# Four one-bank PSUM tiles, in a pool opened after the attention, in place of two two-bank tiles for the first product of an MLP

## The chip, the core and the metric

The kernel runs on one core of a Trainium2 chip. TensorE (PE) multiplies, VectorE (DVE) and ScalarE (ACT) do the elementwise work, GpSimd (POOL) and SyncE (SP) issue transfers. The metric is device time in microseconds, as the median of several runs; a profile is one execution of the same program, read instruction by instruction.

## The reference, cut to what matters

```python
def _attn_ref(u, v, z):                       # u, v: (4, 3008, 256), z: (4, 3008, 64)
    scores = (1.0 / S) * np.matmul(z, z.transpose(0, 2, 1))
    attn = np.maximum(scores, 0.0) ** 2
    return u * np.matmul(attn, v)

def _moe_ref(x, w_in, w_out):                 # x: (12032, 256), w_in: (256, 2048), w_out: (2048, 256)
    h = x @ w_in
    g = np.where(h > 0.0, h, np.exp(np.minimum(h, 0.0)) - 1.0)
    return g @ w_out
```

The result of the attention is the input of the MLP.

## The kernel before

Every matrix product is done in three fp32r products of high and low parts (high by high, high by low, low by high). The kernel has two stages on the same engines.

The **attention** takes 288 steps. It writes its scores alternately into two PSUM tiles, `banks[0]` and `banks[1]` (f0 and f1 in the trace, L120); each is 128 x 2 x 512 numbers of 4 bytes, which is two PSUM banks. Four more tiles of one bank each, `accs` (acc), hold the sums over the steps (L121). That makes eight banks, all there are.

The **MLP** takes 96 steps, in 12 groups of 8. A group has the tokens of two blocks side by side: groups 0, 3, 6 and 9 work on 512 columns, the other eight on 496. A step makes two 128-row slices of the hidden layer for both blocks at once by a scheme with seven products in place of eight (`PARTS`), so it has seven first products M1 to M7 of three matmuls each (L508), and eight second products y0 to y7 of three matmuls each (L525 to L527): 45 matmuls.

The MLP takes over the four banks of f0 and f1. `chain` (L495) says which: p is one half of f0, the other half in the next step; q is the first half of f1 and r the second. In one step:

- p takes M1, then M6, M7 and M4 are added to it. ACT copies p out after each of the four: `s1`, `d`, `u3`, `C21` (all L133).
- q takes M2. DVE adds it in `C11` (L583).
- r takes M5; DVE reads that in `C22` (L585). Then M3 is added to r, and DVE reads the sum in `C12` (L587).

From the four results h, of 4 x 496 columns, ACT makes `m` (L589), `T` (L591) and `E` (L593), DVE makes `tt` (L595) and `max` (L597) and splits the hidden layer into parts with `hi` (L602) and `lo` (L130); the y products read those.

The order on each engine is written out by hand, in `PERIOD` with a lag in steps for each entry, and kept as written (`manual_schedule`). It gives, with t the step of the loop:

- PE: M1(t), y4, y0, M2(t), y1, M6(t), M5(t), y2, y6, M7(t), y7, y5, M4(t), y3, M3(t), the y being those of step t-3.
- DVE: C12(t-1), max(t-2), hi(t-2), lo(t-2), C22(t), C11(t), tt(t-1).
- ACT: s1(t), m(t-1), d(t), T(t-1), u3(t), E(t-1), C21(t).

So C12 of the last step stands behind M2 of this one in the program. Waits between engines are made by the framework, tile by tile: an instruction that reads or writes a tile waits for the earlier ones that wrote or read that tile.

The inputs of the MLP come back from DRAM through POOL's queue (L471), three of the seven tiles of a group in the last step of the group before. Step 1 of the MLP also holds the last work of the attention: DVE finishes the last block and splits seven tiles (L449, L450) between max and C11.

Of the kernel before, what the change touches and what calls it, by code (L numbers as in the profile page):

```python
# [7 lines left out]
F32 = mybir.dt.float32  # L8
# [26 lines left out]
def relu2_attention_elu_mlp(  # L35
# [13 lines left out]
    P = 128  # L49
# [18 lines left out]
    ps = ctx.enter_context(tc.tile_pool(name="ps", bufs=1, space=bass.MemoryType.PSUM))  # L68
# [48 lines left out]
    }  # L117
    H_ROW, M_ROW, T_ROW, G_ROW, L_ROW = ("row3", "row1", "row2"), ("row5",), ("row6",), ("row0", "row8"), ("row7", "row4")

    banks = [ps.tile([P, 2, 512], F32, name=f"f{i}") for i in range(2)]  # L120
    accs = [[ps.tile([P, 512], F32, name=f"acc{i}{h}") for h in range(2)] for i in range(2)]  # L121

    def cols(k):
        return starts[k % NI], BLOCKS[k % NI], k // NI
# [17 lines left out]
    def v_load(b, p):  # L142
        t = st_ring.next().rearrange("p (c d) -> p c d", c=2)
        r0 = 2 * p * P
        if p < NP - 1:
            nc.sync.dma_start(out=t, in_=v[b, r0:r0 + 2 * P, :].rearrange("(c p) d -> p c d", p=P))
        else:
            nc.sync.dma_start(out=t[:, 0, :], in_=v[b, r0:r0 + P, :])
            for h in range(2):
                nc.sync.dma_start(out=t[h * TAIL:(h + 1) * TAIL, 1, :], in_=v[b, r0 + P:S, :])  # L150
        v_raw[b, p] = t

    def v_split(b, p):
        t = v_raw.pop((b, p))
        o = v_ring.next().rearrange("p (q c d) -> p q c d", q=2, c=2)
        if (b, p) == (0, 1):
            nc.vector.tensor_copy(out=o[:, 0], in_=t)
            sub(o[:, 1], t, o[:, 0])
        else:
            split(o[:, 0], o[:, 1], t)  # L160
        v_t[b, p] = o
# [5 lines left out]
    def l_load(b, g):  # L167
        t = l_raw[b, g] = lr_ring.next()
        i0, n = g * GP * 2 * P, GP
        if g == NG - 1:  # L170
            n -= 1
            e = (NP - 1) * 2 * P
            nc.sync.dma_start(out=t[TOP, n * P:], in_=zz[b, TOP, e:e + P])
            for h in range(2):
                o = n * P + h * TAIL
                nc.sync.dma_start(out=t[BOT, o:o + TAIL], in_=zz[b, BOT, e + P:S])
        src = zz[b, :, i0:i0 + n * 2 * P].rearrange("p (n two w) -> p n two w", two=2, w=P)
        for c, rows in enumerate((TOP, BOT)):
            nc.sync.dma_start(out=t[rows, :n * P].rearrange("p (n w) -> p n w", w=P), in_=src[rows, :, c])
# [12 lines left out]
    def r_load(k):  # L192
        i0, n, b = cols(k)
        t = rraw_ring.next()
        nc.sync.dma_start(out=t[:, :n], in_=zz[b, :, i0:i0 + n])
        r_raw[k] = t
# [138 lines left out]
    def a_front(s):  # L335
        k, p = divmod(s, NP)
        n, b = cols(k)[1:]
        hh, ll = (t[:, :n] for t in r_t[k])
        if s < 2:

            w = [[t[:, (2 * p + c) * P:][:, :P] for c in range(2)] for t in (hh, ll)]
        else:
            o = (p % GP) * P
            w = [[t[:, o:o + P]] * 2 for t in l_t[b, p // GP]]
        f_t[s] = banks[s % 2]
        outs = [f_t[s][:, c, :n] for c in range(2)]
        for i in range(3):
            both(outs, w[i % 2], [ll if i == 2 else hh] * 2, i == 0, YES if i == 2 else NO)
# [32 lines left out]
    def a_back(s, part=slice(None)):  # L381
        k, p = divmod(s, NP)
        n, b = cols(k)[1:]
        hi, lo = (t[:, :, :n] for t in e_t[s])
        vt = v_t[b, p]
        last = p == NP - 1
        if p == 0:
            acc_t[k] = accs
        acc = [[h[:, :n] for h in t] for t in acc_t[k]]

        def w(q, c, d):
            return vt[:, q // 2, c, d * P:(d + 1) * P]

        for c, d, q in products(s < 4, p in (0, NP - 1))[part]:
            if not (last and c == 1):
                x = (lo if q == 1 else hi)[:, c]
                both(acc[d], [w(q, c, d)] * 2, (x, x), p == 0 and c == 0 and q == 0, NO)
            elif q == 0:

                both(acc[d], [w(0, 1, d)] * 2, (hi[:, 1], lo[:, 1]), False, (d == 1, True))  # L400
                if d == 0:
                    both((acc[0][0], acc[1][1]), (w(2, 1, 0), w(2, 1, 1)), [hi[:, 1]] * 2, False, (True, False))
# [55 lines left out]
    def x_slots(j):  # L458
        if j == 0:
            x_t[0], spare[0] = list(range(7)), list(range(7, NX))  # L460
        else:
            x_t[j] = spare[j - 1] + x_t[j - 1][:7 - EARLY]
            spare[j] = x_t[j - 1][7 - EARLY:]
# [30 lines left out]

    def chain(s):  # L495
        n = cols(2 * (s // MS))[1]
        return banks[0][:, s % 2, :n], banks[1][:, 0, :n], banks[1][:, 1, :n]

    def m_part(s, name):
        j, m = divmod(s, MS)  # L500
# [168 lines left out]
    def start_up():  # L669
        warm = hi_ring.next()[:, :512]  # L670
        nc.vector.memset(warm.bitcast(F32), 0.0)
        copy(lo_ring.next()[:, :1], warm[:, :1].bitcast(F32))
        f = banks[0]
        for i in range(WARM):
            both([f[:, c] for c in range(2)], [warm[:, :P]] * 2, [warm] * 2, True, YES)
        hh, ll = r_t[0] = r_tiles(0)
        z0 = r_raw.pop(0)
        nc.vector.tensor_copy(out=hh, in_=z0)
        sub(ll, z0, hh)

    with tc.manual_schedule():
        for j in range(NSUP):
            x_slots(j)
        r_load(0)
        v_load(0, 0)
        l_load(0, 0)
        v_load(0, 1)
        l_load(0, 1)
        v_load(0, 2)
        start_up()  # L690
        v_split(0, 0)
        for t in range(NSTEP):

            k, p = divmod(t, NP)
            if not (k and p == 3) and t != 2:
                a_front(t)
            if k and p == 2:
                a_front(t + 1)
            if t >= 2:
                a_back(t - 2)  # L700
            if t == 2:

                a_front(t)
            a_mid(t)
            if t == 0:
                l_hi(0, 0)
                l_lo(0, 0)
            background(t)
        assert not jobs, sorted(jobs)
        for t in range(MSTEP):  # L710
            for name, lag in PERIOD:
                s = t - lag
                if t == 0:
                    if name == "M6":
                        a_back(NSTEP - 2, slice(6, 12))
                    elif name == "M2":
                        a_back(NSTEP - 2, slice(0, 6))
                    elif name == "M7":
                        a_back(NSTEP - 1, slice(0, 6))
                    elif name == "M4":  # L720
                        a_back(NSTEP - 1, slice(6, 12))
                if s < 0:
                    continue
                m_op(s, name)
                if t == 1 and name == "s1":
                    a_sums(NBLK - 1)
                if t == 1 and name == "C12":
                    a_out(NBLK - 1)
                    j = NSUP - 1
                    for _ in x_parts(j):  # L730
                        pass
                    next(late[1], None)
                    for i in range(7):
                        x_split(j, i, scalar=False)
                j = t // MS + 1
                if t % MS == MS - 1 and name == "M2" and j < NSUP:
                    for i in range(EARLY, EARLY + 2):
                        x_load(j, i)
                if t % MS == MS - 1 and name == "M6" and j < NSUP:
                    for i in range(EARLY + 2, 7):  # L740
                        x_load(j, i)
            if t % MS == 4 and t // MS + 1 < NSUP:
                for i in range(EARLY):
                    x_load(t // MS + 1, i)
        s = MSTEP - 1
        m_op(s, "C12")
        m_op(s - 1, "max")
        for half in (1, 0):
            for name in ("m", "T", "E"):
                m_op(s, name, half)  # L750
        for i in Y_ORDER:
            y_part(s - 2, i)
        m_op(s - 1, "hi")
        m_op(s - 1, "lo")
        for i in Y_ORDER:
            y_part(s - 1, i)
        m_op(s, "tt", 1)
        m_op(s, "max", 1)
        m_op(s, "hi", 1, scalar=True)
        m_op(s, "tt", 0)  # L760
        m_op(s, "lo", 1)
        m_op(s, "max", 0)
        m_op(s, "hi", 0, scalar=True)
        m_op(s, "lo", 0)
        for i in Y_LAST:
            y_part(s, i)
            if i < 4:
                y_out(s, i)
# [32 lines left out]
```

## Time and profile before

| | us |
|---|---|
| median of 3 runs (2079.28 to 2081.58) | 2079.36 |
| the profiled execution, its own time | 2082.21 |
| its span, first to last instruction | 2080.4 |
| PE busy over the span | 2004.1 (96%) |
| DVE busy | 1727.8 (83%) |
| ACT busy | 1439.3 (69%) |
| POOL busy | 51.1 (2%) |

The attention fills about the first 965 us, the MLP the rest. The chain of work that ended last lies for 60% of the span on PE and for 37% on DVE. In the rows below, a matmul's record starts when it starts; its end is modelled, so that records of neighbours overlap, and the distance of two starts tells how fast matmuls follow each other. A bracket at the end of a row is the time for which the engine sat idle just before, and what ended that.

### The profile page before, as it was taken

Reading aid. Unit: us, or ns where it says so; the run is one execution under the profiler, and the core shown is the slowest. Engines: PE = TensorE matmul, PEld = TensorE weight load, DVE = VectorE, ACT = ScalarE, POOL = GpSimd, SP = SyncE. Lnnn points to the kernel's source line nnn. Section 1 sums busy time; section 2 is a strip of 40 time slices with the busy share of each in tenths; the row PEclk is TensorE's granted clock in tenths of the full one; section 3 lists DMA queues with packets and bytes.
Section 4 is the critical chain, followed back from the end, with each engine's and each line's share of the span. In section 5 each row is a group of like instructions: output and inputs, shape, how many; then the busy total and the mean of one; then the engine's idle time right before and its main releaser. Section 6 shows DMA issues by size and latency. Waiting matters only on the chain.

```text
span 2080.4 us, 30855 instructions
## 1 busy us (share of the span) xinstructions
PE 2004.1 (96%) x12828; PEld 1592.4 (77%) x12828; DVE 1727.8 (83%) x1726; ACT 1439.3 (69%) x1520; POOL 51.1 (2%) x88
## 2 busy tenths in 40 slices
PE   9999999999999999998899999999999999999998
PEld 7888888888888888886677777777777777777776
DVE  7888888888788888676788888888888888888887
ACT  7666876677676777675567667676676766766665
POOL 0000000000000000001000000000000000000000
PEclk9999999999999999999899999999999999999999
DMA  3132332143131421225011121111221111122100
GB/s 117 44 104 95 96 115 81 56 135 110 56 121 45 131 84 46 71 75 165 33 30 60 50 71 59 30 60 30 71 73 36 60 30 61 31 80 69 30 20 20
DMA packets 76460, 143.16 MB, mean 69 GB/s; under 512 B 7456, under 2 KB 50208, under 8 KB 76320
## 3 DMA queue, kind: packets, MB, share of 16 engines
q1 hardware_dynamic: 63936, 97.56, 14.2%
q0 software_dynamic: 12096, 43.13, 7.0%
q8 instruction: 100, 1.64, 0.3%
q10 hardware_dynamic: 288, 0.51, 0.1%
q14 instruction: 40, 0.33, 0.0%
HBM read 85.72 MB, written 55.44 MB: 68 GB/s over the span
## 4 chain that ended last, share of the span: by engine, by line
PE 60%; DVE 37%; issue 2%; ACT 1%; DMA 0%; ACTq 0%; DVEq 0%
PE acc L333 34%; DVE row L130 12%; PE f L508 11%; DVE row L597 10%; PE f L333 8%; DVE row L602 6%; DVE row L587 3%; DVE row L583 3%; DVE row L585 3%; PE acc L525 2%; PE acc L526 2%; PE acc L527 2%; DVE row L375 1%; ACT row L374 1%; DVE row L420 1%
## 5 line engine op out<-in xcount | busy, mean ns | idle before, releaser
L333 PE MATMUL acc<-row,x 64*128 64x496 f32 (+1 forms) x6768 | 806.3, 384 | 4.6 <-DVE row L130 4.4
L333 PEld LDWEIGHTS acc<-row,x 64*128 64x128 f32 x6768 | 633.5, 184 | 135.1 <-DVE row L130 9.2
L130 DVE TENSOR_TENSOR row<-row,row 128x992 fp32r<-128x992 f32 (+7 forms) x464 | 613.6, 1326 | 17.2 <-ACT row L133 1.2
L371 ACT ACTIVATE row<-f 128x992 f32<-128x992 f32 (+1 forms) x287 | 289.5, 1009 | 240.9 <-PE f L333 219.0
L133 ACT ACTIVATE row<-f 128x496 f32<-128x496 f32 (+1 forms) x384 | 222.8, 580 | 157.9 <-PE f L508 155.8
L589 ACT ACTIVATE row<-row 128x1984 f32<-128x1984 f32 (+2 forms) x97 | 181.1, 1867 | 197.1 <-DVE row L587 194.9
L375 DVE CAST row<-row 128x992 fp32r<-128x992 f32 (+1 forms) x287 | 195.3, 681 | 135.4 <-ACT row L374 135.3
L374 ACT ACTIVATE row<-row 128x992 f32<-128x992 f32 (+1 forms) x287 | 299.3, 1043 | 8.4
L526 PE MATMUL acc<-row,wo_hi 128*128 128x496 f32 (+1 forms) x768 | 298.8, 389 | 1.8 <-DVE row L130 1.8
L525 PE MATMUL acc<-row,wo_hi 128*128 128x496 f32 (+1 forms) x768 | 299.0, 389 | 0.0
L527 PE MATMUL acc<-row,wo_lo 128*128 128x496 f32 (+1 forms) x768 | 298.6, 389 | 0.0
L508 PE MATMUL f<-x,wi_hi 128*128 128x496 f32 (+1 forms) x768 | 259.1, 419 | 4.9 <-ACT row L133 4.6
L597 DVE SCALAR_TENSOR_TENSOR row<-row,row 128x1984 f32<-128x1984 f32 (+2 forms) x97 | 215.0, 2216 | 0.0
L595 DVE SCALAR_TENSOR_TENSOR row<-row,row 128x1984 f32<-128x1984 f32 (+2 forms) x97 | 214.8, 2214 | 0.0
L508 PEld LDWEIGHTS f<-x,wi_hi 128*128 128x128 f32 x768 | 130.8, 190 | 81.4 <-ACT row L133 66.2
L587 DVE TENSOR_TENSOR row<-f,row 128x496 f32<-128x496 f32 (+1 forms) x96 | 65.3, 680 | 152.4 <-PE f L508 152.4
L591 ACT ACTIVATE row<-row 128x1984 f32<-128x1984 f32 (+2 forms) x97 | 180.0, 1856 | 1.8 <-DVE row L597 1.7
L593 ACT ACTIVATE row<-row 128x1984 f32<-128x1984 f32 (+2 forms) x97 | 180.7, 1863 | 0.1
L526 PEld LDWEIGHTS acc<-row,wo_hi 128*128 128x128 f32 x768 | 145.1, 189 | 31.2 <-DVE row L130 2.1
L525 PEld LDWEIGHTS acc<-row,wo_hi 128*128 128x128 f32 x768 | 144.8, 188 | 30.2 <-DVE row L602 0.2
L527 PEld LDWEIGHTS acc<-row,wo_lo 128*128 128x128 f32 x768 | 145.0, 189 | 29.0
L508 PE MATMUL f<-x,wi_lo 128*128 128x496 f32 (+1 forms) x384 | 150.4, 392 | 0.0
(71 smaller groups left out, 1587.1 us busy)
## 6 DMA issues: line engine op xcount, KB each, us to landing
x<-x POOLq DMA_DIRECT2D x56, 496.0 KB, 4.6
x<-row SPq DMA_DIRECT2D x84, 248.0 KB, 2.0
x<-x POOLq DMA_DIRECT2D x28, 512.0 KB, 4.7
row<-in_v SPq DMA_DIRECT2D x44, 256.0 KB, 2.8
x<-row SPq DMA_DIRECT2D x42, 256.0 KB, 2.1
row<-in_uT SPq DMA_DIRECT2D x16, 496.0 KB, 4.0
x<-high SPq DMA_DIRECT2D x28, 248.0 KB, 2.0
outT<-x SPq DMA_DIRECT2D x14, 496.0 KB, 3.7
```

The source lines that it names most:

```text
L130: nc.vector.tensor_tensor(out=lo, in0=src, in1=hi.bitcast(F32), op=ALU.subtract)
L133: nc.scalar.activation(out=out, in_=in_, func=AF.Copy)
L333: nc.tensor.matmul(out, w[rows], x[rows], start=start, stop=end)
L371: nc.scalar.activation(out=x, in_=f[:, c, :n], func=AF.Relu, scale=1.0 / S)
L374: nc.scalar.activation(out=x, in_=x, func=AF.Square)
L375: nc.vector.tensor_copy(out=hi[:, c, :n], in_=x)
L508: nc.tensor.matmul(o, w, x, start=first and i == 0, stop=i == 2, skip_group_check=not first)
L525: nc.tensor.matmul(o, wh, hi, start=first, stop=False)
L526: nc.tensor.matmul(o, wh, lo, start=False, stop=False)
L527: nc.tensor.matmul(o, wl, hi, start=False, stop=last)
L595: stt(out=t, in0=m, scalar=1.0, in1=t, op0=ALU.add, op1=ALU.mult)
L597: stt(out=h, in0=h, scalar=0.0, in1=t, op0=ALU.max, op1=ALU.add)
```

## The change

The two-bank tiles of the scores come from a pool of their own, which is closed when the attention's loop is done. A new pool is opened there with four tiles of one bank: p0 and p1 (p of even and of odd steps), q and r. They lie on the same four banks and are used in the same way. No instruction is added or removed on an engine, and none changes its place; lines behind L120 move down by two or three.

```diff
-    banks = [ps.tile([P, 2, 512], F32, name=f"f{i}") for i in range(2)]
+    scores = ExitStack()
+    fs = scores.enter_context(tc.tile_pool(name="fs", bufs=1, space=bass.MemoryType.PSUM))
+    banks = [fs.tile([P, 2, 512], F32, name=f"f{i}") for i in range(2)]
...
     def chain(s):
         n = cols(2 * (s // MS))[1]
-        return banks[0][:, s % 2, :n], banks[1][:, 0, :n], banks[1][:, 1, :n]
+        p0, p1, q, r = singles
+        return (p1 if s % 2 else p0)[:, :n], q[:, :n], r[:, :n]
...
         assert not jobs, sorted(jobs)
+        scores.close()
+        fm = ctx.enter_context(tc.tile_pool(name="fm", bufs=1, space=bass.MemoryType.PSUM))
+        singles = [fm.tile([P, 512], F32, name=name) for name in ("p0", "p1", "q", "r")]
         for t in range(MSTEP):
```

What differs is who waits for whom. These are PE's rows from M3 of one step to M2 of the next, in the MLP with 496 columns; a name in brackets is the semaphore of the engine that is waited for (DVE_49 is DVE's, Activation_49 ACT's). Before:

```order
L508 MATMUL f1_98<-x2_11188,x11_10821 128x496 [waits DVE_49]
L508 MATMUL f1_98<-x2_11188,x11_10821 128x496 x2
L508 MATMUL f0_97<-x7_11036,wi_hi_63 128x496 [waits Activation_49]
L508 MATMUL f0_97<-x7_11036,wi_hi_63 128x496
L508 MATMUL f0_97<-x7_11036,wi_lo_64 128x496
L525 MATMUL acc00_99<-row0_10896,wo_hi_65 128x496
L526 MATMUL acc00_99<-row7_10902,wo_hi_65 128x496
L527 MATMUL acc00_99<-row0_10896,wo_lo_66 128x496
L525 MATMUL acc00_99<-row0_10896,wo_hi_65 128x496
L526 MATMUL acc00_99<-row7_10902,wo_hi_65 128x496
L527 MATMUL acc00_99<-row0_10896,wo_lo_66 128x496
L508 MATMUL f1_98<-x8_11038,wi_hi_63 128x496 x2
```

And in the changed kernel:

```order
L511 MATMUL r_10741<-x2_11199,x11_10832 128x496 [waits DVE_49]
L511 MATMUL r_10741<-x2_11199,x11_10832 128x496 x2
L511 MATMUL p1_10739<-x7_11047,wi_hi_63 128x496 x2
L511 MATMUL p1_10739<-x7_11047,wi_lo_64 128x496
L528 MATMUL acc00_102<-row0_10907,wo_hi_65 128x496
L529 MATMUL acc00_102<-row7_10913,wo_hi_65 128x496
L530 MATMUL acc00_102<-row0_10907,wo_lo_66 128x496
L528 MATMUL acc00_102<-row0_10907,wo_hi_65 128x496
L529 MATMUL acc00_102<-row7_10913,wo_hi_65 128x496
L530 MATMUL acc00_102<-row0_10907,wo_lo_66 128x496
L511 MATMUL q_10740<-x8_11049,wi_hi_63 128x496 [waits DVE_49]
L511 MATMUL q_10740<-x8_11049,wi_hi_63 128x496
```

M1 has lost a wait on ACT and M2 has gained one on DVE. Two waits keep their semaphore and change the count that they ask for, in all 96 steps of the built program: M3 asks for the count of C22 of its step, where it asked for that of C11, one instruction later on DVE. C12 of step t-1 asks PE for the third matmul of M3(t-1), where it asked for the third of M2(t), which stands twelve matmuls further on.

## Rows read from the trace of the kernel before

**Rows 1.** Busy time by stretch: attention, the MLP's first steps (two), the steady MLP.

```profile
core 0: us, PE busy (x) PEld busy (x) DVE busy (x) ACT busy (x) POOL busy (x), PEclk, DMA share, GB/s
500.00:960.00 460.00, 457.79 (x4074) 381.27 (x4072) 372.60 (x476) 330.45 (x375) 5.15 (x9) 1.00 0.28 89
975.00:980.00 5.00, 2.27 (x8) 0.97 (x6) 4.17 (x7) 4.01 (x6) 0.00 (x0) 0.96 0.01 2
980.00:985.00 5.00, 3.30 (x6) 1.66 (x6) 4.52 (x10) 4.81 (x5) 0.00 (x0) 0.50 0.35 131
1100.00:1400.00 300.00, 286.19 (x1202) 219.38 (x1202) 255.28 (x187) 203.95 (x199) 15.88 (x25) 1.00 0.18 57
```

**Rows 2.** Waits, 1400 to 1700 us: who for whom; us in total, times, longest.

```profile
DVE row L587 <- PE f L508: 42.8, 27, 1.6
```

**Rows 3.** Timeline, one 496-column step: start, us, engine, line, operation, count, idle before.

```profile
1402.57 0.95 PE L508 MATMUL f<-x,x 128*128 128x496 f32 x3 [0.52 <-DVE row L583]
...
1404.04 0.39 PE L525 MATMUL acc<-row,wo_hi 128*128 128x496 f32 x1
...
1405.83 0.39 PE L508 MATMUL f<-x,wi_lo 128*128 128x496 f32 x1
...
1406.26 0.68 DVE L587 TENSOR_TENSOR row<-f,row 128x496 f32<-128x496 f32 x1 [1.61 <-PE f L508]
...
1408.80 0.56 ACT L133 ACTIVATE row<-f 128x496 f32<-128x496 f32 x1
...
1409.21 0.38 PE L527 MATMUL acc<-row,wo_lo 128*128 128x496 f32 x1
...
1411.01 0.57 ACT L133 ACTIVATE row<-f 128x496 f32<-128x496 f32 x1
...
1411.47 1.86 ACT L593 ACTIVATE row<-row 128x1984 f32<-128x1984 f32 x1
1411.64 0.72 PE L508 MATMUL f<-x,wi_hi 128*128 128x496 f32 x2
...
1412.47 0.67 DVE L585 TENSOR_TENSOR row<-f,row 128x496 f32<-128x496 f32 x1
...
1413.06 0.66 DVE L583 TENSOR_TENSOR row<-f,row 128x496 f32<-128x496 f32 x1
...
1413.64 2.21 DVE L595 SCALAR_TENSOR_TENSOR row<-row,row 128x1984 f32<-128x1984 f32 x1
...
1413.78 0.94 PE L508 MATMUL f<-x,x 128*128 128x496 f32 x3 [0.52 <-DVE row L583]
...
1417.43 0.68 DVE L587 TENSOR_TENSOR row<-f,row 128x496 f32<-128x496 f32 x1 [1.58 <-PE f L508]
```

**Rows 4.** Timeline, one step with 512 columns.

```profile
1289.07 0.96 PE L508 MATMUL f<-x,wt 128*128 128x512 f32 x3 [0.55 <-DVE row L583]
...
1290.56 0.39 PE L525 MATMUL acc<-row,wo_hi 128*128 128x512 f32 x1
...
1292.80 0.69 DVE L587 TENSOR_TENSOR row<-f,row 128x512 f32<-128x512 f32 x1 [1.59 <-PE f L508]
...
1295.78 0.39 PE L527 MATMUL acc<-row,wo_lo 128*128 128x512 f32 x1
...
1300.53 0.74 PE L508 MATMUL f<-x,x 128*128 128x512 f32 x2 [0.55 <-DVE row L583]
```

**Rows 5.** Timeline of PE: M3 of step 3 and M3 of the last step, 95.

```profile
1018.55 0.96 PE L508 MATMUL f<-x,wt 128*128 128x512 f32 x3 [0.54 <-DVE row L583]
...
2055.55 0.94 PE L508 MATMUL f<-x,x 128*128 128x496 f32 x3 [0.55 <-DVE row L583]
```

**Rows 6.** Waits, 960 to 1022 us (the MLP's steps 0 to 3).

```profile
DVE row L587 <- PE f L508: 6.5, 2, 4.4
```

**Rows 7.** Last load of a group on POOL's queue; median time to landing of such loads.

```profile
1419.03 0.53 POOL L471 DMA_DIRECT2D x<-x  x1 [0.82 <-PE f L508]
...
x<-x POOLq DMA_DIRECT2D x28, 512.0 KB, 4.7
```

## The prediction, written before the changed kernel ran

> **What bounds the kernel now.** I began with the busy times by stretch [rows 1]. In the attention PE is busy for 457.79 of 460 us, so nothing there depends on a wait, and the change leaves it alone but for its end. In the steady MLP PE is busy for 286.19 of 300 us, DVE for 255.28 and ACT for 203.95: no engine is full, so a chain through several of them must set the pace. The waits name it: DVE's C12 (L587) waits for a first product of PE (L508) in each of the 27 steps between 1400 and 1700 us, 42.8 us in all or 1.6 us a time [rows 2].
>
> One step of the timeline closes the loop [rows 3]. C12 starts at 1406.26, C11 (L583) ends at 1413.06 + 0.66 = 1413.72, 7.46 us later, and DVE pauses nowhere between. M3 starts at 1413.78; its bracket says that it waited for C11. Then PE does M3, M1, y4, y0 and M2, fifteen matmuls, and the next C12 starts at 1417.43, 3.65 us after M3. Together 7.46 + 0.06 + 3.65 = 11.17 us, which is the length of a step. C12 to C11 on DVE, M3 to M2 on PE, and round again.
>
> Both links are false. M3 writes r, and C11 reads q; C12 reads r, whose last product M3 ended at 1402.57 + 0.95 = 1403.52, yet it starts only at 1406.26, just behind the end of M2's last matmul (1405.83 + 0.39 = 1406.22) [rows 3]. M2 writes q. Since q and r are halves of one tile, each is waited for on account of the other. Step by step, PE waits until DVE is done with q, and DVE waits until PE has rewritten q.
>
> **What the change removes.** With q and r in tiles of their own, the built program has M3 ask for C22 and C12 ask for M3. The loop above is cut at both places. What is next, and how long is a step then?
>
> PE by itself: matmuls follow each other undisturbed from y4's first at 1404.04 to y6's last at 1409.21, which is 23 distances in 5.17 us, 0.2248 us each [rows 3]. 45 of them are 10.12 us. With 512 columns the same stretch runs from 1290.56 to 1295.78, 0.2270 us each, 10.21 us a step, against 1300.53 - 1289.07 = 11.46 now [rows 4].
>
> DVE by itself: a step less its only wait, 11.17 - 1.58 = 9.59 us [rows 3], with 512 columns 11.46 - 1.59 = 9.87 us [rows 4].
>
> ACT and DVE in a ring: C12 is followed on ACT by m, d, T, u3, E, and E by tt on DVE, which stands ahead of the next C12. From C12 at 1406.26 to E's end at 1411.47 + 1.86 = 1413.33, then 0.06 to be seen and 2.21 for tt [rows 3]: 9.34 us.
>
> So PE would be the slowest, if it waits for nothing. I check its waits with M3 at 0 and matmul number i at 0.2248 i, all distances from [rows 3]. M7 (number 30) starts at 6.74, its third ends at 7.58, u3 ends 0.04 + 0.57 later at 8.19. M4 (number 39, at 8.77) needs u3: 0.5 us to spare. C22 needs u3 too: 8.25 to 8.92; the next M3 at 10.12 needs C22: 1.1 to spare. C11 ends at 9.50; M2 (at 10.12 + 12 x 0.2248 - 0.67 = 12.1) carries the wait that is new, on C11: 2.6 to spare, and what is queued behind it on PE is not held up. E starts 0.46 after u3 (1411.47 against 1411.01), at 8.08, and ends at 9.94; tt, which could start at 9.5, waits half a microsecond for it, 10.0 to 12.2. C12 then comes 2.1 us after the next M3. M5 (at 4.72 after its M3) rewrites r and needs C12, done at 2.8: 1.9 to spare. d comes 1408.80 - 1406.26 = 2.54 behind C12 and takes 0.56: done at 5.2, M7 wants it at 6.74. All hold. DVE and ACT have moved back by some 1.6 us against PE, and PE no longer stops.
>
> The other waits: M1 loses a wait on ACT that was long over when M1 followed M3. The pool's closing and opening fall in one place, where PE has attention matmuls between the first products of step 0; I count nothing. Group ends have four more copies on ACT, but its 203.95 of 300 us [rows 1], 7.7 us a step with these copies in, stay below 10.1: nothing. The loads: the last of a group is issued at 1419.03 and lands some 4.7 us later [rows 7]; M3 of the next step, which reads it, starts at about 1424.95 + 11.2 = 1436.1. Of 12 us to spare a faster step takes about two.
>
> **The sum.** From M3 of step 3 at 1018.55 to M3 of step 95 at 2055.55 are 92 steps in 1037.0 us [rows 5], 28 with 512 columns and 64 with 496. After: 28 x 10.21 + 64 x 10.12 = 285.9 + 647.7 = 933.6. Gain 103.4 us.
>
> The first steps are another matter. There DVE also splits the last tiles, PE is busy for 2.27 of 5 us, and its granted clock falls from full (2.4 GHz) to 0.50 (1.2 GHz) [rows 1]. The same false wait costs 6.5 us there in two steps [rows 6]; but at the half clock PE itself may be what bounds them. Between 0 and 6.5 I take 3, the middle, since nothing is nearer to one end. The tail behind the last M3 has no M2 to wait for: nothing. 103.4 + 3 = 106 us. The profiled execution took 2082.21 with a span of 2080.4; that is 1974 for the span, and set against the median of the runs, 2079.36 - 106 = **1973**. I round to 1974, with a trifle for the 11 group ends.
>
> On the profile's face the gain looks smaller. PE's idle time is 13.81 of 300 us [rows 1], which over 1037 us is 48. The brackets say the same: 0.52 before M3 [rows 3]. But a record covers 0.39 us where the next matmul could have started 0.2248 after, so a stall shows 0.17 too short, and the first matmul after it is itself slower. The distances of starts hold nothing of this, and I go by them.
> The Trainium skill, page "Trainium Kernel Development and Optimization", section "Performance Expectations", has a rule for that: matmul busy time is a bad metric, because matmuls are pipelined, and the share of weight loading is a better one. By it the 48 us are no ceiling; by the busy row they are. Here the starts agree with the rule: 11.17 a step against 45 x 0.2248.
>
> **The rivals.**
>
> *Only the idle time shown comes back.* If something that I don't see holds matmuls apart once they are dense, the gain is the 48 us of idle records: 2031. Against it, the 23 undisturbed distances already are dense. 4%.
>
> *DVE or ACT becomes the bound.* With 512 columns DVE's 9.87 is within 4% of PE's 10.21, and M4 has only 0.5 us to spare behind u3. If ACT or DVE runs a few per cent slower beside an unbroken PE, or their order meshes less well than my frame, 0.3 us a step comes back, 28 us in 92 steps: 2002. For it: the tight places. Against it: DVE and ACT do the same instructions on the same banks. 11%.
>
> *The clock.* PE without a pause could be granted less. At the half clock a step is 20.2 us; each microsecond in it loses half a one, and 212 us of it, a fifth of the MLP, eat the gain. With a quarter of the MLP's 960 us at the half clock the time is 1974 + 120 = 2094, slower than before. Against it: in the attention PE is busier than it would be here, 457.79 of 460, at a clock of 1.00, and the clock fell where PE was busy for 2.27 of 5 us [rows 1]. 3%.
>
> *The change doesn't do what it says.* If the waits had been by bank all along, nothing changes: 2079. The row of C12 behind M2 [rows 3] speaks against that plainly. 2%.
>
> **How the numbers follow.** The forecast, 1974, has 80%; its own range is 1964 to 1990: 3.5 us less if the first steps give all of the 6.5, and some more if the half clock there is not granted at all; 16 us more for residues of 0.1 to 0.2 us a step. To leave out no more than 2 in 10 the range reaches over the second rival: 1964 to 2008. A measurement of this kernel can tell about 0.2%, 4 us, from no change. Faster: forecast, shown idle time and second rival, 95%; the same: 2%; slower: 3%.
>
> **What would show it.** Right: C12's wait for PE is gone and tt waits for E (ACT) about half a microsecond; PE has no bracket before M3; M3 follows M3 after 10.1 us with 496 columns and 10.2 with 512; the steady MLP has DVE near 95% busy; the clock there stays at 1.00. Wrong: steps of 10.3 or more with a bracket before M4 or M7 (ACT), or before M3 or M5 (DVE); a clock under 1.00 behind 1021 us; M2 waiting for C11; PE waiting for a load at a group's first steps.

## The result, and the profile after

| us | before | after |
|---|---|---|
| median | 2079.35 | 1968.92 |
| ratio after to before, 95% interval | | 0.946 [0.9442, 0.9479] |
| profiled execution, its own time | 2082.21 | 1969.42 |
| its span | 2080.4 | 1967.6 |
| forecast, with its range | | 1974 (1964 to 2008) |

One of the four executions of the changed kernel took 3952.84 us, for a reason that no trace here shows; the median has it in, the ratio leaves it out.

The changed kernel is 110 us faster, 5.4%. The page of its profile, engines' busy time first (PEld is PE's weight load), then the chain of work that ended last:

```profile
PE 1941.4 (99%) x12828; PEld 1611.5 (82%) x12828; DVE 1728.5 (88%) x1726; ACT 1456.7 (74%) x1520; POOL 50.9 (3%) x88
...
PE 94%; DVE 4%; issue 1%; ACT 1%; DMA 0%; ACTq 0%; DVEq 0%
```

DVE has done the same work (1728.5 us against 1727.8) in a shorter time, and the chain has become PE almost alone: 94% where it was PE 60% and DVE 37%. The steady MLP, in the same columns as [rows 1]:

```profile
1100.00:1400.00 300.00, 300.00 (x1337) 250.76 (x1336) 285.20 (x209) 231.51 (x221) 14.79 (x24) 1.00 0.17 52
```

1337 matmuls in 300 us where there were 1202, without an idle record, at the full clock. What waits there are, from 1100 to 1900 us (who for whom; us in total, times, longest; POOL left out):

```profile
ACT row L135 <- PE p L511: 120.3, 192, 1.3
ACT row L592 <- DVE row L590: 46.2, 69, 1.0
DVE row L598 <- ACT row L596: 33.2, 79, 0.5
ACT x L135 <- PE acc L530: 7.6, 10, 0.8
```

C12 (now L590) waits for nobody, where [rows 2] had 1.6 us a step. DVE's only wait left is tt (L598) for E (L596), and PE has none at all. One step with 496 columns:

```profile
1356.40 2.23 DVE L598 SCALAR_TENSOR_TENSOR row<-row,row 128x1984 f32<-128x1984 f32 x1 [0.45 <-ACT row L596]
1356.53 0.83 PE L511 MATMUL r<-x,x 128*128 128x496 f32 x3
1357.20 0.61 PE L511 MATMUL p<-x,wi_hi 128*128 128x496 f32 x2
...
1357.87 0.38 PE L528 MATMUL acc<-row,wo_hi 128*128 128x496 f32 x1
...
1358.54 0.67 DVE L590 TENSOR_TENSOR row<-r,row 128x496 f32<-128x496 f32 x1
...
1359.20 0.61 PE L511 MATMUL q<-x,wi_hi 128*128 128x496 f32 x2
...
1362.98 0.39 PE L530 MATMUL acc<-row,wo_lo 128*128 128x496 f32 x1
...
1364.56 1.85 ACT L596 ACTIVATE row<-row 128x1984 f32<-128x1984 f32 x1
1364.75 0.67 DVE L588 TENSOR_TENSOR row<-r,row 128x496 f32<-128x496 f32 x1
...
1365.33 0.66 DVE L586 TENSOR_TENSOR row<-q,row 128x496 f32<-128x496 f32 x1
...
1366.31 0.57 ACT L135 ACTIVATE row<-p 128x496 f32<-128x496 f32 x1
...
1366.44 2.23 DVE L598 SCALAR_TENSOR_TENSOR row<-row,row 128x1984 f32<-128x1984 f32 x1 [0.45 <-ACT row L596]
1366.58 0.83 PE L511 MATMUL r<-x,x 128*128 128x496 f32 x3
```

M3 follows M3 after 10.05 us, without a bracket, where [rows 3] had 11.2 and one of 0.52. C12 starts 2.01 us behind M3 (forecast: 2.1) and now ahead of the next M2, which it used to wait for. C22 is over 1.16 us before M3 needs it (forecast: 1.1).

### The profile page after: what moved, and what is told of

Same layout as the page of the kernel before. It is cut to its first block, busy times and chain, and to the rows that moved or that the text cites. A ratio compares the mean times of both kernels' runs of the same rounds, so it can differ in the third digit from the quotient of the medians.

```text
span 1967.6 us, 30854 instructions
## 1 busy us (share of the span) xinstructions
PE 1941.4 (99%) x12828; PEld 1611.5 (82%) x12828; DVE 1728.5 (88%) x1726; ACT 1456.7 (74%) x1520; POOL 50.9 (3%) x88
## 4 chain that ended last, share of the span: by engine, by line
PE 94%; DVE 4%; issue 1%; ACT 1%; DMA 0%; ACTq 0%; DVEq 0%
PE acc L335 36%; PE p L511 13%; PE f L335 9%; PE acc L528 9%; PE acc L530 9%; PE acc L529 9%; PE r L511 6%; PE q L511 3%; DVE row L132 2%; DVE row L377 1%; ACT row L376 1%; DVE row L422 1%; DMA x<-row 0%; DVE row L598 0%; DVE row L600 0%
## 5 line engine op out<-in xcount | busy, mean ns | idle before, releaser
L135 ACT ACTIVATE row<-p 128x496 f32<-128x496 f32 (+1 forms) x384 | 226.0, 588 | 168.5 <-PE p L511 162.7
L598 DVE SCALAR_TENSOR_TENSOR row<-row,row 128x1984 f32<-128x1984 f32 (+2 forms) x97 | 215.9, 2226 | 38.9 <-ACT row L596 38.9
L511 PE MATMUL p<-x,wi_hi 128*128 128x496 f32 (+1 forms) x576 | 178.6, 391 | 4.7 <-ACT row L135 4.7
L596 ACT ACTIVATE row<-row 128x1984 f32<-128x1984 f32 (+2 forms) x97 | 180.1, 1857 | 0.1
L511 PEld LDWEIGHTS p<-x,wi_hi 128*128 128x128 f32 x576 | 108.4, 189 | 28.4 <-ACT row L135 6.9
L605 DVE CAST row<-row 128x1984 fp32r<-128x1984 f32 (+1 forms) x95 | 114.5, 1205 | 3.3
L335 PE MATMUL f<-q,row 64*128 64x496 f32 (+1 forms) x852 | 116.5, 383 | 0.0
```

Of the source, the lines that this page charges most:

```text
L135: nc.scalar.activation(out=out, in_=in_, func=AF.Copy)
L335: nc.tensor.matmul(out, w[rows], x[rows], start=start, stop=end)
L511: nc.tensor.matmul(o, w, x, start=first and i == 0, stop=i == 2, skip_group_check=not first)
L598: stt(out=t, in0=m, scalar=1.0, in1=t, op0=ALU.add, op1=ALU.mult)
```

## The experiments

All runs of a table row have the kernel before beside them on the same chip; ratios are to it.

| kernel | median us | ratio, 95% interval |
|---|---|---|
| only q and r in tiles of their own | 1970.83 | 0.9472 [0.9458, 0.9486] |
| only p's halves in tiles of their own | 2080.78 | 1.0 [0.9991, 1.0009] |
| tiles of before, C12 ahead of M2 in the program | 1990.11 | 0.9564 [0.9548, 0.958] |
| tiles of before, M3 ahead of C11 | 2037.12 | 0.9792 [0.9777, 0.9806] |
| changed kernel again | 1968.55 | 0.9459 [0.9446, 0.9472] |
| changed, a quarter of hi twice | 1970.53 | 0.947 [0.9457, 0.9483] |
| changed, the whole of hi twice | 2040.34 | 0.9805 [0.9792, 0.9819] |
| changed, ACT copies for the last tiles, five buffers | 1969.16 | 0.9465 [0.9452, 0.9478] |
| the same, seven buffers | 1964.07 | 0.944 [0.9427, 0.9453] |
| changed kernel beside the last | 1968.58 | 0.9461 [0.9448, 0.9474] |

**Which of the two separations counts.** The first kernel leaves p in a two-bank tile:

```diff
-    banks = [fs.tile([P, 2, 512], F32, name=f"f{i}") for i in range(2)]
+    banks = [(ps if i == 0 else fs).tile([P, 2, 512], F32, name=f"f{i}") for i in range(2)]
...
-        p0, p1, q, r = singles
-        return (p1 if s % 2 else p0)[:, :n], q[:, :n], r[:, :n]
+        q, r = singles
+        return banks[0][:, s % 2, :n], q[:, :n], r[:, :n]
...
```

> Only q and r get one-bank tiles; p stays the two halves of one two-bank tile, so M1 of a step again waits for ACT's copy C21 of the step before. Theory (the false tie between q and r is all): M3 has no idle bracket for DVE, steps of 10.05 us with 496 columns as in the changed kernel, 1969 us within 5. Rival (the false tie between p's halves counts too, since ACT is now later against PE): in the changed kernel E ends at 1364.56 + 1.85 and C21 (0.57, start 1366.31) ends at 1366.88, while M1 starts at 1367.24, 0.36 us to spare; if ACT slips by more than that in a good part of the steps, 0.1 to 0.2 us a step come back: 1979 to 1988.

The second does the reverse: p0 and p1 are tiles, q and r the halves of `banks[1]`.

> The other half alone: p gets two one-bank tiles, q and r stay halves of one two-bank tile. Theory: the loop C12, C11, M3, M2, C12 is untouched, M1's wait on ACT was long over when M1 followed M3, so steps stay at 11.17 us and the time at 2079, within 2. Rival (p's tie held part of it): a quarter or more of the gain, 2050 or less.

Measured: 1970.83 and 2080.78. The tie between q and r is nearly all of it: with p alone separated, the time is that of before, and the waits from 1100 to 1900 us are the old ones:

```profile
DVE row L590 <- PE f L511: 112.6, 71, 1.7
...
PEld f L511 <- DVE row L586: 67.4, 71, 1.1
```

C12 for M2 and M3 for C11, in each of the 71 steps. With q and r separated and p not, a little is missing: 2.3 us between the medians (1968.55 for the changed kernel), and 3.4 us in the traces, from M3 of step 3 to M3 of step 95 (934.10 against 930.66). It lies at the group ends. In the changed kernel, M3 follows M3 after 10.05 us there too, here after 10.3 to 10.4 (with 496 columns), and the waits of this kernel from 1100 to 1900 us have a line that the changed one lacks:

```profile
PEld f L511 <- ACT row L135: 4.3, 10, 0.5
```

Ten waits in 800 us, one at each group end: ACT copies four accumulators as well, C21 comes late, and M1 has to wait for a copy of the other half of its tile. The rival was right about the mechanism, and wrong about how often it bites.

**The two links of the loop, each cut without touching PSUM.** Here the tiles are those of before. Only the order of recording differs, so that the false wait points the other way; the order on each engine is the same.

```diff
-    ("M1", 0), ("y4", 3), ("s1", 0), ("y0", 3), ("M2", 0), ("ev0", 3), ("C12", 1), ("y1", 3), ("max", 2),
+    ("M1", 0), ("y4", 3), ("s1", 0), ("y0", 3), ("C12", 1), ("M2", 0), ("ev0", 3), ("y1", 3), ("max", 2),
```

> The PSUM tiles are those of the kernel before; in the program C12 of the last step stands ahead of M2 of this one instead of behind it. The order on each engine is the same. C12 then waits for M3 alone, and in return M2 waits for C12; M3 still waits for C11. Theory (false waits set the pace, C12 behind M2 is the expensive one): the loop is cut by this alone. A new ring is left: C12 (0.67 and 0.06) before M2, 20 distances of 0.2233 to M7's third matmul and 0.39 to its end, 0.04, u3 to E 0.46, E 1.86, 0.06, tt 2.21, and C12 again: 0.73 + 4.86 + 0.04 + 0.46 + 1.86 + 0.06 + 2.21 = 10.22, with 0.1 for PE's restart 10.3 us a step against 10.05 after: 1985 to 1995. Rival (the gain comes from something in the tiles or their place, not from the waits): 2079. Rival (both false waits cost the same, so half is left): about 2025.

```diff
-    ("C11", 0), ("M3", 0), ("C21", 0), ("ev3", 3), ("ev1", 3), ("tt", 1),
+    ("M3", 0), ("C11", 0), ("C21", 0), ("ev3", 3), ("ev1", 3), ("tt", 1),
```

> The PSUM tiles are those of the kernel before; in the program M3 stands ahead of C11 instead of behind it. M3 then waits for C22 alone, and in return C11 waits for M3; C12 still waits for M2. Theory: two rings are left. C12 to C22's end is 1412.47 + 0.67 - 1406.26 = 6.88, M3 to the next C12 is 3.71: 10.6. On DVE C22, M3 (0.06 + 0.95 + 0.05), C11 and tt (0.59 + 2.21) and C12: 6.88 + 1.06 + 2.80 = 10.74 us a step, 0.43 less than before: 2038, between 2030 and 2048. Rival (either cut gives the whole gain): 1975 or less. Rival (a tie through the tiles' place, not through waits): 2079.

Measured: 1990.11 and 2037.12, both in the ranges of the theory, and both away from all rivals. In the first, three rows of one step show the new ring, C12 with M2 held back behind it and tt waiting for E:

```profile
1386.18 2.23 DVE L595 SCALAR_TENSOR_TENSOR row<-row,row 128x1984 f32<-128x1984 f32 x1 [0.50 <-ACT row L593]
...
1388.33 0.67 DVE L587 TENSOR_TENSOR row<-f,row 128x496 f32<-128x496 f32 x1
...
1389.04 0.30 PEld L508 LDWEIGHTS f<-x,wi_hi 128*128 128x128 f32 x2 [0.31 <-DVE row L587]
```

Within a group, steps with 496 columns are 10.22 to 10.27 us there; I had 10.22, and 10.3 with 0.1 for PE's restart, which turns out cheaper. In the second, the new wait is C11's for M3, from 1100 to 1900 us:

```profile
DVE row L583 <- PE f L508: 77.2, 74, 1.1
```

1.04 us in each step, with steps of 10.63 us against 10.74 worked out. So the effect follows from who waits for whom. Nothing is left over for the pools or the place of the banks: these two runs change neither, and the kernel with p alone separated has the new pool and no gain. The wait of C12 for M2 was the dearer link: cutting it alone gives 89 of the 110 us, cutting the other alone 42. The two sum to more than the whole; as I read it, each cut ends at a ring that is left, and behind both stand PE's own 45 matmuls.

**Is PE now the only bound?** To measure the slack on DVE rather than to read it off the idle time, hi is done again, for a quarter of its columns and for all of them:

```diff
                 nc.vector.tensor_copy(out=g, in_=h)
+                if half is None:
+                    nc.vector.tensor_copy(out=g[:, :n], in_=h[:, :n])
```

> The changed kernel once more, beside the three others on one chip, so that they have it for comparison: 1969 within 3 us by every theory.

> The changed kernel with one more DVE instruction in each step but the last two: behind hi a second copy of its first quarter, 128x496, onto the same place, about 0.46 us. Theory (PE alone bounds the step now, and DVE has its 0.45 us of idle ahead of tt to spare): DVE's own step is 9.60 + 0.46 = 10.06 with 496 columns, level with PE's 10.05, and 9.87 + 0.47 = 10.34 with 512, 0.14 over PE's 10.20: 5 to 10 us in 94 steps, 1974 to 1979. Rival (DVE is in the ring that sets the step, its idle time is no slack): 0.46 in each of 94 steps, 43 us, 2012.

> The changed kernel with the whole of hi done twice, about 1.23 us more on DVE in each of 94 steps. Theory: DVE becomes the bound, 9.60 + 1.23 = 10.83 us with 496 columns and 9.87 + 1.27 = 11.14 with 512: 0.78 x 63 + 0.94 x 31 = 78 us, 2047 within 8. The idle time before tt is gone and M3 waits for C22. Rival (DVE was in the ring before): 1.23 x 94 = 116 us, 2085. Rival (there is more slack than the idle time shows): 2010 or less.

Measured: 1968.55 for the changed kernel, 1970.53 with a quarter more, 2040.34 with the whole. The quarter is nearly free. It has used up the idle time, as the waits from 1100 to 1900 us tell:

```profile
DVE row L598 <- ACT row L596: 0.5, 3, 0.2
```

Steps stay at 10.05 and 10.20 us. I had expected 5 to 10 us more, since my DVE step of 9.59 us was too long: I had taken a step of before less its wait, and there C12 follows tt after tt's full 2.21. In the kernel with the quarter, where nothing is waited for, the rows are closer:

```profile
1358.30 2.23 DVE L598 SCALAR_TENSOR_TENSOR row<-row,row 128x1984 f32<-128x1984 f32 x1
1360.44 0.67 DVE L590 TENSOR_TENSOR row<-r,row 128x496 f32<-128x496 f32 x1
```

2.14 us from start to start, so 9.52 a step. With the whole of hi twice, DVE is the bound: 10.73 us a step, and M3 has a bracket again, for C22:

```profile
1383.51 0.94 PE L511 MATMUL r<-x,x 128*128 128x496 f32 x3 [0.37 <-DVE row L588]
```

9.52 + 1.23 = 10.75 agrees. The 1.23 us lengthen the step by 10.73 - 10.05 = 0.68, so DVE has some 0.55 us of slack a step with 496 columns; what goes beyond it counts in full.

**What is left: the first steps.** In the changed kernel PE still waits before M3 of step 1, while DVE splits seven tiles, with its copies into two buffers that must first be stored:

```profile
990.44 1.65 PE L511 MATMUL r<-x,wt 128*128 128x512 f32 x3 [7.57 <-DVE row L588]
```

The next kernel lets ACT do those copies, behind m, into five buffers.

```diff
-                    for i in range(7):
-                        x_split(j, i, scalar=False)
+                if t == 1 and name == "m":
+                    own = [w_hi.next(), w_hi.next()] + [temps[i].bitcast(F32R) for i in range(3)]
+                    for i in range(7):
+                        x_split(NSUP - 1, i, hi=own[i % 5])
```

> The changed kernel with another start of the MLP: in step 1 the high parts of the last group's seven tiles are copied by ACT, behind its m of step 0, and not by DVE, into five buffers in turn instead of two. Theory (in the first steps DVE is the bound and PE waits 7.6 us for it): DVE loses seven copies of 0.42 us and some waits of 0.25 us for buffers, so that C22 of step 1, at 989.7 us in the changed kernel, comes at about 985: 4 to 5 us less, 1964 to 1965, and the half clock is granted for a shorter time or not at all. Rival (the transfers of these tiles, which fill the DMA engines there, or ACT's later d and M7, are the bound): within 2 us of the changed kernel.

Measured: 1969.16, the same as the changed kernel's 1968.55. The rival won, and the timeline of ACT says how: the first copy waits until DVE has read what lay in its buffer, the seventh for a store out of its own, and d and M7 stand behind them.

```profile
981.36 0.62 ACT L135 ACTIVATE row<-row 128x496 fp32r<-128x496 f32 x1 [2.26 <-DVE x L132]
...
986.32 0.62 ACT L135 ACTIVATE high<-row 128x496 fp32r<-128x496 f32 x1 [1.60 <-DMA x<-high]
```

So the last try gives each copy a buffer of its own, two of them in a row of SBUF that is free by then, and takes the one that DVE still reads last:

```diff
+                    own = [w_hi.parts[0], cut(hl[2], 2), cut(hl[2], 3)] + [temps[i].bitcast(F32R) for i in range(4)]
+                    for i in range(7):
+                        x_split(NSUP - 1, i, hi=own[i])
```

> As the start with ACT's copies, but with seven buffers, one for each copy, so that no copy waits for a transfer. Theory (DVE and the waits for two buffers are the bound of the first steps; the last try only moved the wait from DVE to ACT, where 1.60 us for a buffer held back d and with it M7 and u3): copies from 979 to 983 us, d and M7 behind them, C22 of step 1 at about 986 in place of 990 to 991, 4 to 5 us less than the changed kernel, 1964 to 1965. Rival (the 14 transfers, 3.5 MB at the 371 GB/s seen there, are the bound): they end no earlier, and some wait of that kind turns up behind them; within 2 us of the changed kernel.

> The changed kernel beside it on the same chip: 1969 within 3 us.

Measured: 1964.07 (1962.41 to 1966.03) against 1968.58 (1968.02 to 1969.11) of the changed kernel beside it. The 4.5 us expected are there, in the trace too:

```profile
982.83 1.22 PE L511 MATMUL p<-x,wi_hi 128*128 128x512 f32 x2 [5.06 <-ACT row L135]
...
985.14 0.69 DVE L588 TENSOR_TENSOR row<-r,row 128x512 f32<-128x512 f32 x1
```

C22 of step 1 comes at 985.14, against 990.83 in the run beside it; counted from M3 of step 0, 12.93 us behind it against 17.85.

```profile
990.83 0.68 DVE L588 TENSOR_TENSOR row<-r,row 128x512 f32<-128x512 f32 x1
```

The transfers were no bound by themselves; what counted were the waits for a buffer, wherever they stood. This kernel is faster by 0.2% than the changed one beside it. The two sets of times don't overlap, though one execution of the changed kernel in the first comparison took 1965.07.

## Why the prediction was right

**The loop.** Right, in both links: each was cut by itself, and gave what the remaining rings give.

**The new step.** Right in kind, 0.7% long: 10.05 us measured against 10.12 with 496 columns, 10.20 against 10.21 with 512. The term was mis-sized by the distance between matmuls. From y4's first to y6's last took 5.17 us before and takes 1362.98 - 1357.87 = 5.11 after; 45 in 10.05 us are 0.2233 each, where I took 0.2248 from a stretch without a bracket, which I held for undisturbed. Over the 92 steps, from M3 of step 3 to M3 of step 95:

```profile
1012.11 0.84 PE L511 MATMUL r<-x,wt 128*128 128x512 f32 x3
...
1942.77 0.83 PE L511 MATMUL r<-x,x 128*128 128x496 f32 x3
```

930.66 us against 1037.0 [rows 5] and 933.6 forecast: 2.9 us more gain.

**The frame of waits.** Right where it could be seen: tt waits 0.45 us for E (forecast: half a microsecond), C12 comes 2.01 behind M3, no wait stops PE. The new wait of M2 costs nothing. One line was too quick: that M1's lost wait on ACT was worth nothing. At the group ends it is worth 3.4 us, and the four copies there cost nothing only because the halves of p are apart too. With both terms at zero the sum came out right for the changed kernel all the same.

**The first steps.** Under-sized: I took 3 us, between 0 and 6.5, and M3 of step 3 came 1018.55 - 1012.11 = 6.44 us sooner. But 0.96 of that lies ahead of the MLP, in the attention, which the change leaves alone. M1 of step 0, before and after:

```profile
962.25 0.73 PE L508 MATMUL f<-x,wi_hi 128*128 128x512 f32 x2
...
961.29 0.73 PE L511 MATMUL p<-x,wi_hi 128*128 128x512 f32 x2
```

The other 5.48 us are the first steps' own, most of the 6.5 of [rows 6], but not through the wait alone. The granted clock fell to half (1.2 GHz) as it had before:

```profile
975.00:980.00 5.00, 2.07 (x7) 0.97 (x6) 4.97 (x10) 4.01 (x4) 0.00 (x0) 0.97 0.00 2
980.00:985.00 5.00, 1.65 (x3) 0.83 (x3) 4.24 (x10) 3.50 (x4) 0.00 (x0) 0.50 0.60 223
```

But it was back sooner. From 1005 to 1010 us PE was busy throughout in both kernels, before at half the clock with 13 matmuls, after at the full one with 24:

```profile
1005.00:1010.00 5.00, 5.00 (x13) 3.84 (x12) 1.43 (x1) 0.60 (x1) 0.00 (x0) 0.50 0.00 0
...
1005.00:1010.00 5.00, 5.00 (x24) 4.14 (x23) 4.29 (x3) 3.42 (x4) 0.00 (x0) 1.00 0.00 0
```

So PE at the half clock had its part in these steps, as I had thought it might. What it costs shows between two executions of the changed kernel: M3 of step 2 started at 1000.23 at half the clock in the first, where M3 of step 3 followed after 11.88 us (14.26 before), and at the full clock when the kernel ran again, where it took 10.37:

```profile
1000.23 1.65 PE L511 MATMUL r<-x,wt 128*128 128x512 f32 x3 [0.63 <-DVE row L588]
...
1001.38 0.98 PE L511 MATMUL r<-x,wt 128*128 128x512 f32 x3 [0.37 <-DVE row L588]
...
1011.75 0.84 PE L511 MATMUL r<-x,wt 128*128 128x512 f32 x3
```

How the 5.48 us divide between the wait and the clock stays open. The two mis-sized terms, 2.9 for the step and 2.5 here, and the 1.0 from the attention make up the 6.4 us between the 106.4 of the sum and 112.8 in the spans. The tail was untouched: 2080.4 - 2055.55 = 24.85 us before, 1967.6 - 1942.77 = 24.83 after.

**The rivals.** "Only the idle time shown", 2031, fell: 110 us came back where 48 were shown as idle. The rule that I had set beside it (the Trainium skill, page "Trainium Kernel Development and Optimization", section "Performance Expectations": matmul busy time is a bad metric, the share of weight loading a better one) agrees with this trace, though not to the figure: the matmuls went from 1202 to 1337 in 300 us, up by 11%, PE's busy time by only 5%, that of weight loading by 14%, from 219.38 to 250.76. "DVE or ACT becomes the bound" fell by a margin that the added copies measured, some 0.5 us a step. "The clock" fell: 1.00 in the steady MLP with PE busy throughout. That the waits were by bank all along fell with the first trace.

## What to carry to other kernels

In this kernel a wait on PSUM was made for the whole two-bank tile, not for the numbers touched: two accumulators in one such tile were tied to each other's readers and writers, and the trace shows it as a wait of an instruction for one that writes something it doesn't read. The rule that I gave for all waits, tile by tile, is too wide, though. C11 and then C21 write two quarters of one row in SBUF, and in the kernel before C21 starts while C11 [rows 3] still runs, from 1413.06 to 1413.72:

```profile
1413.23 0.58 ACT L133 ACTIVATE row<-f 128x496 f32<-128x496 f32 x1
```

So read from the trace which tiles are tied. Look for such pairs wherever a chain passes between engines at each step, and cut them by splitting the tile, or, where there is no room, by recording the reader ahead of the unrelated writer; that turns the wait round, and here left 21 us of the gain behind. And take what a stall costs from the distances of starts, since idle records showed less than half of it here.

## What the runs showed of the hardware

Matmuls of 128 x 128 weights on 496 columns followed each other after 0.2233 us once nothing interrupted them, a little closer than in the stretch of before that had no bracket either (0.2248; the same stretch after, 0.2222). I can't say from these runs what the rest was.

At half the clock 13 matmuls, all on 512 columns and without a pause, filled 5 us; at the full clock 24 did.

Two DVE instructions that depend on nothing outstanding start closer than the first one's record is long: 2.14 us apart behind a record of 2.23, and 0.58 (C22 and C11) behind one of 0.67.
